# Attention and gated MLP on one core: bias rows mirrored in the matmul, splits and some relus given to POOL, and a new instruction order planned with a corrected count

## The chip, the cores and the metric

The kernel runs on one core of one Trainium2 chip. That core has five engines with their own instruction queues: TensorE (PE in the profile, its weight loads PEld), VectorE (DVE), ScalarE (ACT), GpSimd (POOL) and SyncE (SP, which issues DMA transfers here). They share the on-chip memory SBUF; matmul results land in PSUM. The metric is device time in microseconds of one execution, lower is better. Three timed runs of the kernel before gave 770.35, 771.11 and 771.43 us.

## What is computed

Eight batches, eight heads, 576 positions, head size 64. Attention with a position bias from a small two-layer network, then a gated MLP over the 512 joined channels. Cut to what matters:

```python
scores = scale * np.matmul(q, k.transpose(0, 1, 3, 2))
psi_rel = np.log1p(np.abs(rel)); psi_i = np.log1p(np.maximum(pos[:, None], 1.0))
h = np.maximum((psi_rel / psi_i)[..., None] @ w1 + b1, 0.0)      # 32 hidden
scores = scores + (h @ w2).transpose(2, 0, 1)[None]              # a bias per head
attn = softmax(scores);  x = attn @ v                            # heads joined to 512 channels
gate = sigmoid(causal 5-tap convolution of x, per channel)
out = (gate * (x @ w_val)) @ w_out
```

The bias of row i at column j depends on |i - j| and on i alone, so a row of it is a function of the distance, laid out forwards from the diagonal and backwards before it.

## The kernel before

**An order worked out on the host.** Nothing is scheduled by hand or by a compiler. While the kernel is built, every piece of work is entered as a task with `add`: the engines that may do it with a cost for each, a priority, the tasks it needs, and the buffers it takes and uses. `Plan.order` then plays the program through in a model of the five engines, and emits the tasks in the order that this gives, each on the engine that the model chose. What steers it are tables of numbers at the top of the file: `PAIR_AT` and `MLP_AT` (when a pair of heads, or an MLP, is due), `OFFS` (priority by kind of task), `LOOK` (how far a task may jump the queue for a buffer), `LOAD` (how an engine's time is weighed). `RUNS` sets in which order the 32 pairs (two heads of a batch) come. For TensorE the model also counts instructions: `INSTR` holds how many each kind of task issues, and each time the count passes `BLOCK` = 256 the model lets TensorE wait until a block of instructions has been fetched.

**Bias rows** (`bias_rows`, 36 calls, m = 0 to 35, 16 rows i each). Four `relu` tasks (ACT L348, DVE or POOL L350) make the hidden layer for the w distances that these rows need (288 to 576). `bias_mm` (L370) multiplies it in TensorE, four 32-row groups side by side, in one or two column pieces. `bias_fin` (ACT L390, DVE L392) takes each piece out of PSUM into `t_be` once forwards and once backwards (a reversed output pattern), two to four evictions for each m. `bias_store` sends `t_be` to DRAM, from where `bias_ld` (L442, L446) reads it skewed, so that the bias of a chunk of 128 rows is in place.

**Pairs** (`pair`, 32). For each of five chunks of rows: `qkm` or `qkr` (PE L843, L863) makes scores, `logits` (DVE L714) adds the bias and takes the minimum, `expo` (ACT L727), `eps`, `recip`, and `norm` (POOL L740). Then the weights are turned: for the first four pairs by TensorE (`tp`, `tpr`, `tpe`, evicted by ACT or DVE copies L260, L262), for the others by DVE (`turn_`, L887, L889). `av` (PE L944) multiplies with v in three tasks of 48 matmuls; a matmul of 32-bit operands is two matmuls and two weight loads in the trace, so such a task is 96 of each. `ev` (L268, L270) moves the result to `xp`.

**MLPs** (`mlp`, 8, one for each batch when its four pairs are done). `conv` and `sig` make the gate. In two parts of positions (256 and 320): `split_hi` (L260, L262, L264) and `split_lo` (L273) split x into two 16-bit numbers, `val` (PE L1082, three groups of four matmuls for each of four column blocks), `gf` (DVE L1092), `ghi` and `glo` (L260 to L264 and L273) split the gated product, `outp` (PE L1145), `ote`, and a store.

**Scales.** `wm_fin` takes the maxima of both weight matrices on DVE (`all_max`, once for each), and `vm_fin` those of v for each batch.

Of the kernel before, what the change touches and what calls it, by code (L numbers as in the profile page):

```python
# [50 lines left out]
INSTR = dict(qkm=16, qkr=32, av=192, bias_mm=16, val=8, outp=8, vm_sum=4, tp=16, tpr=4, tpe=10, avt=16)  # L51
# [167 lines left out]
def attention_gated_mlp(  # L219
# [105 lines left out]
    def bias_rows(m):  # L325
# [7 lines left out]
        cuts = (0, w) if w <= 512 else (0, w // 2, w)  # L333
# [31 lines left out]
        def bias_mm(e, j):  # L365
            if j == 0:
                new(pb, [P, 2, 512], F32)
            x, y = pieces[j]
            for g in range(4):
                T.matmul(  # L370
                    pb.t[32 * g : 32 * g + 32, j, 0 : y - x],
                    lhsT=w28,
                    rhs=rel[g].t[:, x:y],
                    start=True,
                    stop=True,
                    tile_position=(0, 32 * g),
                )

        def bias_fin(e, j, lo, hi, back):
            if j == 0 and not back:  # L380
                new(be, [P, S + 16], F32)
            x = pieces[j][0]
            i = pb.t[:, j, lo - x : hi - x]
# [1 line left out]
            if back:
                o = be.t[:, wb - hi : wb - lo][:, ::-1]
            else:
                o = be.t[:, wb - 1 + lo : wb - 1 + hi]
# [5 lines left out]
        fs, bs = [], []  # L394
        first = t = None
        for j, (x, y) in enumerate(pieces):
            t = add([("P", 0.1 + 0.5 * (y - x) / HS)], partial(bias_mm, j=j), rts + [t], pri + 0.3, [pb] if j == 0 else (), [rel[0]])
            for back, n, l in ((False, wf, fs), (True, wb, bs)):
                lo, hi = max(x, 1 if back else 0), min(y, n)
                if lo >= hi:  # L400
                    continue
# [855 lines left out]
```

## Time and profile before

| | |
|---|---|
| timed runs | 770.35, 771.11, 771.43 us; median 771.11 |
| the profiled execution | 773.37 us, of which the span from first to last instruction is 771.6 |
| busy in that span | PE 642.9, DVE 614.3, ACT 561.6, POOL 483.5 us |
| mean granted TensorE clock | 0.957 of full |
| DMA | 142 MB, 184 GB/s |

A busy time is the union of an engine's instructions. "Idle before, releaser" says how long the engine stood idle just before a group, and what ended it; "issue" as the releaser means that the profile shows nothing that the engine waited for. The program has three parts: some 70 us in which the bias rows are made, a stretch to about 280 us in which the weights are prepared and the first pairs run, and then the steady work, with the last pair's `av` ending at 729.4 us and the last MLP behind it.

### The profile page before, as it was taken

What the parts mean: (1) busy time and instruction counts of PE and PEld (TensorE: products, weight loads), DVE (VectorE), ACT (ScalarE), POOL (GpSimd) and SP (SyncE); (2) the same over time, 40 slices, a digit from 0 to 9 for tenths busy, and PEclk for the clock granted to TensorE, in tenths of its full rate; (3) what the DMA queues carried; (4) which work ended last, traced back from release to release, by engine and by line L of the source; (5) the groups of instructions that cost most, each with busy time, mean ns of one, the idle gap of its engine ahead of it and who ended that gap; (6) DMA issues with size and microseconds to landing.
All of it is one profiled execution on the core that took longest, in us unless ns stands there. A gap on an engine that the chain in (4) does not pass through costs nothing. (4 is left out here: it accounts for less than half of the span.)

```text
span 771.6 us, 27070 instructions
## 1 busy us (share of the span) xinstructions
PE 642.9 (83%) x11244; PEld 403.6 (52%) x11244; DVE 614.3 (80%) x1392; ACT 561.6 (73%) x1315; POOL 483.5 (63%) x567
## 2 busy tenths in 40 slices
PE   5667898878577899898988899899889999778976
PEld 1123555455364556565565475557546565555643
DVE  6998889898976779979886988879688896977420
ACT  6998787878755587879757876788488485677532
POOL 0200568786953795869867777768588377667541
PEclk9899999986888999999999999999999999899999
DMA  8999955694576455773768147654764456920011
GB/s 276 308 341 299 304 183 181 216 280 131 162 252 179 131 177 152 216 230 100 236 199 256 43 137 233 224 190 125 242 203 146 144 171 204 287 84 16 17 56 41
DMA packets 57642, 142.15 MB, mean 184 GB/s; under 512 B 6192, under 2 KB 6960, under 8 KB 57520
## 3 DMA queue, kind: packets, MB, share of 16 engines
q1 hardware_dynamic: 52272, 130.99, 54.1%
q10 hardware_dynamic: 5248, 9.44, 3.5%
q8 instruction: 88, 1.44, 0.8%
q14 instruction: 34, 0.28, 0.1%
HBM read 120.08 MB, written 20.33 MB: 182 GB/s over the span
## 5 line engine op out<-in xcount | busy, mean ns | idle before, releaser
L740 POOL TENSOR_SCALAR t_d<-t_d,rinv 128x576 f32<-128x576 f32 x256 | 201.3, 800 | 133.6 <-DVE rinv L736 129.6
L727 ACT ACTIVATE t_d<-t_d,nm 128x576 f32<-128x576 f32 x256 | 196.3, 767 | 54.6 <-DVE nm L714 41.5
L714 DVE CUSTOM_DVE_ANT_0 t_d<-t_sp,bias 128x576 f32<-128x576 f32 x256 | 186.3, 743 | 24.9 <-PE t_sp L843 21.2
L843 PE MATMUL t_sp<-t_qk 64*128 64x288 f32 x1024 | 169.4, 447 | 36.2 <-DVE nm L714 22.8
L944 PE MATMUL t_sp<-t_pt,t_vx 32*64 32x128 f32 (+1 forms) x8064 | 166.4, 301 | 27.5 <-issue 19.9
L944 PEld LDWEIGHTS t_sp<-t_pt,t_vx 32*64 32x64 f32 x8064 | 144.8, 135 | 54.9 <-issue 39.3
L887 DVE STREAM_TRANSPOSE t_pt<-t_d 128x1152 f32<-128x1152 f32 x112 | 152.0, 1365 | 12.8 <-POOL t_d L740 6.5
L1022 POOL TENSOR_TENSOR t_w<-t_w 128x576 f32<-128x576 f32 x96 | 136.8, 1429 | 14.1 <-ACT t_w L1017 7.9
L843 PEld LDWEIGHTS t_sp<-t_qk 64*128 64x128 f32 x1024 | 96.4, 195 | 90.4 <-DVE nm L714 33.8
L1082 PEld LDWEIGHTS <-wv 128*128 128x128 f16 x768 | 72.2, 99 | 48.4 <-issue 30.6
L1082 PE MATMUL t_sp<-xh,wv 128*128 128x320 f16 (+1 forms) x512 | 79.0, 291 | 7.9 <-DVE t_w L1092 4.9
L1145 PE MATMUL t_sp<-wo,gh 128*128 128x512 f16 x256 | 64.8, 385 | 12.8 <-ACT t_w L268 7.5
L268 ACT ACTIVATE xp<-t_sp,xsc 128x256 f32<-128x256 f32 (+1 forms) x108 | 38.6, 391 | 49.4 <-PE t_sp L944 45.5
L1092 DVE SCALAR_TENSOR_TENSOR t_w<-t_sp,wrel,t_w 128x256 f32<-128x256 f32 (+1 forms) x64 | 32.5, 510 | 41.4 <-PE t_sp L1082 36.0
L370 PE MATMUL t_sp<-rel,w 128*32 128x288 f32 (+17 forms) x352 | 44.0, 540 | 20.7 <-ACT t_be L390 11.0
L1017 ACT ACTIVATE t_w<-xp,convb 128x576 f32<-128x576 f32 x74 | 55.4, 767 | 5.3 <-DMA out<-t_w 2.5
L273 POOL TENSOR_TENSOR gl<-t_w,gh 128x256 f16<-128x256 f32 x48 | 33.0, 690 | 32.1 <-ACT gh L260 26.4
L1145 PEld LDWEIGHTS <-gh 128*128 128x128 f16 x256 | 23.5, 99 | 47.8 <-issue 18.8
L727 ACT ACTIVATION_READ_ACCUMULATOR t_d<-t_d,nm 128x1 f32 x256 | 47.9, 187 | 0.0
L348 ACT ACTIVATE rel<-gt,b1t,sct 128x432 f32<-128x432 f32 (+17 forms) x69 | 47.5, 763 | 0.0
L733 ACT ACTIVATE rinv<-sm,epst 128x2 f32<-128x2 f32 (+1 forms) x160 | 44.3, 287 | 1.8 <-ACT t_d L727 0.4
L1082 PE MATMUL t_sp<-xl,wv 128*128 128x256 f16 (+1 forms) x256 | 42.6, 289 | 2.6 <-DVE t_w L1092 1.9
(128 smaller groups left out, 833.4 us busy)
## 6 DMA issues: line engine op xcount, KB each, us to landing
bias<-bias_d SPq DMA_DIRECT2D x72, 576.0 KB, 5.5
t_vx<-vr SPq DMA_DIRECT2D x84, 384.0 KB, 3.7
t_qk<-qkd SPq DMA_DIRECT2D x32, 576.0 KB, 4.8
bias_d<-t_be SPq DMA_DIRECT2D x36, 295.5 KB, 4.8
t_vx<-vf SPq DMA_DIRECT2D x24, 384.0 KB, 3.6
out<-t_w ACTq DMA_DIRECT2D x32, 256.0 KB, 2.2
biasr<-bias_d SPq DMA_DIRECT2D x36, 144.0 KB, 6.7
t_d<-wvd SPq DMA_DIRECT2D x4, 512.0 KB, 6.7
```

Of the source, the lines that this page charges most:

```text
L348: A.activation(out=rel[g].t[:, 0:w], in_=src, func=AF.Relu, bias=b1t, scale=sct[:, mm : mm + 1])
L714: V.tensor_tensor_reduce(out=eb.t[:, a * S : (a + 1) * S].rearrange("p (j f) -> p j f", j=2), in0=sps[a].t[:, :, 0:HS], in1=bias.rearrange ...
L727: A.activation(out=x, in_=x, func=AF.Exp, bias=st["nm"][:, a : a + 1], scale=-1.0, accum_out=st["sm"][:, a : a + 1])
L733: A.activation(out=st["r"][:, 0:heads], in_=st["sm"][:, 0:heads], func=AF.Identity, bias=epst)
L740: (G if e == "G" else V).tensor_scalar(out=t, in0=t, scalar1=st["r"][:, a : a + 1], scalar2=1.0, op0=ALU.mult, op1=ALU.mult)
L843: T.matmul(ts[a][:, j, 0:HS], lhsT=qk.t[r, c * P : (c + 1) * P], rhs=qk.t[r, S + j * HS : S + (j + 1) * HS], start=True, stop=True,)
L887: V.transpose(out=x[:, c : 9 - c : 8 - 2 * c, :], in_=eb.t.rearrange("p (a f) -> p a f", a=2))
L944: T.matmul(avs[i // 2].t[o, i % 2, 0 : 32 * k], lhsT=vxs[j0 // 6].t[r, j - j0, o], rhs=pv[r, 0:k, j, :] if a == 0 else pv[r, 8 : 8 - k : - ...
L1017: A.activation(out=tmp.t, in_=x, func=AF.Copy, scale=cw)
L1022: (V if e == "V" else G).tensor_tensor(out=gates[k].t, in0=gates[k].t, in1=tmp.t, op=ALU.add)
L1082: T.matmul(pm.t[:, d % 2, 0:w], lhsT=pools["wv"][wi][:, k, d * P : (d + 1) * P], rhs=xb.t[xi][:, k, 0:w], start=(q == 0 and k == 0), stop= ...
L1145: T.matmul(pm.t[:, y, :], lhsT=gb.t[gi][:, k, o : o + P] if o < 256 else gx.t[gi][:, k, :], rhs=pools["wo"][wi][:, k, :], start=(q == 0 an ...
```

## The change

It has these parts.

1. `bias_mm` writes the whole row of 592 columns to PSUM, the backward half by reading `rel` with a reversed pattern (`[:, ::-1]`), in three or four pieces (`cuts`), and one `bias_fin` evicts it whole.
2. Every fourth m gives its fourth `relu` to POOL alone (`ON_G`), and POOL's modelled cost falls from 2.6 to 1.9 us for 576 columns.
3. `INSTR` of the tasks that turn weights on TensorE is raised by a fraction (`tp` 16 to 16.75, and so on): the model's count was short by what they issue besides matmuls and loads.
4. `all_max` takes both weight matrices at once; `vm_fin` makes two scale rows with one instruction (`xsc`, `osc`, `vmx` are laid out for it).
5. Modelled costs of `ev`, `norm`, `wm_fin`, `vm_fin` are altered, `av` and `ev` get a due time of their own (`PAIR_B`), so does the second part of an MLP (`MLP_B`), and all tables are set anew. With that the whole order is another.

```diff
-PAIR_AT = (12, -16, -1, -7.5, -6.5, -5.5, 7.5, -19.5, 9, -8, -4.5, 2.5, 3.5, 2, -3, -4.5, -4, 2.5, 2.5, -2.5, 3.5, -8.5, -5.5, -8.5, -3, -7, -2, -21.5, -19.5, -2.5, -2.5, 20)
+PAIR_AT = (15, -17.5, 2, -11.5, -6.5, -24, -8.5, -5, 10, -17, -4.5, -3.5, -8.5, 4, 8.5, 5.5, 0.5, -1.5, -4.5, -13.5, -13, -2.5, -2.5, -6, -4.5, -12, -10, -15.5, -4.5, 13, 29, 24.5)
...
-INSTR = dict(qkm=16, qkr=32, av=192, bias_mm=16, val=8, outp=8, vm_sum=4, tp=16, tpr=4, tpe=10, avt=16)
+INSTR = dict(qkm=16, qkr=32, av=192, bias_mm=16, val=8, outp=8, vm_sum=4, tp=16.75, tpr=4.75, tpe=10.75, avt=16.45)
...
-LOAD = dict(P=0.8, V=1.07, A=0.48, G=0.68, S=1.61)
+LOAD = dict(P=0.49, V=2, A=0.74, G=1.15, S=1.8)
...
+ON_G = tuple(range(0, 36, 4))
...
-        cuts = (0, w) if w <= 512 else (0, w // 2, w)
+        left = int(wf > wb)
+        mid = wb - 1 + left
+        cuts = sorted({0, mid, SPLIT, 2 * SPLIT})
...
-            eng = [("A", 0.22 + 0.54 * w / S), ("V", 0.1 + 0.4 * w / S), ("G", 0.15 + 2.6 * w / S)]
+            eng = [("A", 0.22 + 0.54 * w / S), ("V", 0.1 + 0.4 * w / S), ("G", 0.15 + 1.9 * w / S)]
+            if g == 3 and m in ON_G:
+                eng = eng[2:]
...
+        def bias_mm(e):
+            new(pb, [P, 2, 512], F32)
+            for x, y in pieces:
+                if y <= mid:
+                    lo, hi = mid - y + 1, mid - x + 1
+                else:
+                    lo, hi = x - mid, y - mid
+                for g in range(4):
+                    r = rel[g].t[:, lo:hi]
+                    T.matmul(
+                        pb.t[32 * g : 32 * g + 32, x // SPLIT, x % SPLIT : x % SPLIT + y - x],
+                        lhsT=w28,
+                        rhs=r[:, ::-1] if y <= mid else r,
...
+        t = add([("P", 0.1 + 0.04 * len(pieces) + 1.03)], bias_mm, rts, pri + 0.3, [pb], [rel[0]], times=len(pieces))
+        f = add([("A", 0.59), ("V", 0.72)], bias_fin, [t], pri + 0.5, [be], [pb])
...
-        for x in range(2):
-            V.tensor_reduce(out=wall[:, x : x + 1], in_=i[:, x], op=ALU.max, axis=AX.X)
-            all_max(wall[:, x : x + 1])
+        V.tensor_reduce(out=wall[:, 0:2], in_=i, op=ALU.max, axis=AX.X)
+        all_max(wall[:, 0:2])
...
-                ta = add([("P", 1.62)], partial(av, j0=j0), turned + [tvs[j0 // 6], ta], s0 + 13, () if ta else avs, u)
+                ta = add([("P", 1.62)], partial(av, j0=j0), turned + [tvs[j0 // 6], ta], s0 + 13 + PAIR_B[n], () if ta else avs, u)
...
-            base = st + (12 + 9 * pi) * per
+            base = st + (12 + 9 * pi) * per + pi * MLP_B[done]
```

What the order makes of it is shown at three places. Line numbers of the changed kernel are about ten lower than before: its L354 and L356 are `relu`, L396 and L398 `bias_fin`, L717 `expo`, L730 `norm`, L277 the splits, L833 `qkm`, L934 `av`, L1135 `outp`.

The first is ACT's queue where the bias rows end and the first softmax begins; `t_be` is a bias row on its way to DRAM, `t_d` a chunk of weights. Before:

```order
L348 ACTIVATE rel<-gt,b1t,sct 128x560
L348 ACTIVATE rel<-gt,b1t,sct 128x576
L390 ACTIVATE t_be<-t_sp,cadd 128x80
L348 ACTIVATE rel<-gt,b1t,sct 128x576
L390 ACTIVATE t_be<-t_sp,cadd 128x511
L390 ACTIVATE t_be<-t_sp,cadd 128x264
L390 ACTIVATE t_be<-t_sp,cadd 128x271
L390 ACTIVATE t_be<-t_sp,cadd 128x279
L390 ACTIVATE t_be<-t_sp,cadd 128x16
L390 ACTIVATE t_be<-t_sp,cadd 128x287
L727 ACTIVATE t_d,sm<-t_d,nm 128x576 x3
L733 ACTIVATE rinv<-sm,epst 128x2
```

Now:

```order
L396 ACTIVATE t_be<-t_sp,cadd 128x592
L354 ACTIVATE rel<-gt,b1t,sct 128x528 x2
L354 ACTIVATE rel<-gt,b1t,sct 128x544 x2
L717 ACTIVATE t_d,sm<-t_d,nm 128x576
L354 ACTIVATE rel<-gt,b1t,sct 128x560 x2
L354 ACTIVATE rel<-gt,b1t,sct 128x576
L717 ACTIVATE t_d,sm<-t_d,nm 128x576
L354 ACTIVATE rel<-gt,b1t,sct 128x576
L723 ACTIVATE rinv<-sm,epst 128x2
L717 ACTIVATE t_d,sm<-t_d,nm 128x576 x3
L723 ACTIVATE rinv<-sm,epst 128x2
L396 ACTIVATE t_be<-t_sp,cadd 128x592
```

The first five exponentials stand ahead of ACT's last bias eviction, among its last rectifications, where before all of the bias work came first.

The second is TensorE's queue late in the program, between the pairs that come 29th and 30th: `t_pt` are turned weights, `t_vx` is v, `gh` an MLP's gated product. An `av` run of two tasks is 73 rows that alternate between two widths, of which the last three or four are shown. Before:

```order
L944 MATMUL t_sp<-t_pt,t_vx 64x160 x2
L944 MATMUL t_sp<-t_pt,t_vx 64x128
L944 MATMUL t_sp<-t_pt,t_vx 64x160
L944 MATMUL t_sp<-t_pt,t_vx 64x128
L843 MATMUL t_sp<-t_qk 128x288 x12
L944 MATMUL t_sp<-t_pt,t_vx 64x160
L944 MATMUL t_sp<-t_pt,t_vx 64x128
```

Now, behind the run of two `av` tasks of the 30th pair:

```order
L934 MATMUL t_sp<-t_pt,t_vx 64x160
L934 MATMUL t_sp<-t_pt,t_vx 64x128
L934 MATMUL t_sp<-t_pt,t_vx 64x160
L833 MATMUL t_sp<-t_qk 128x288 x4
L1135 LDWEIGHTS gh
L1135 MATMUL t_sp<-wo_1271,gh 128x512
```

Before, another run of two `av` tasks followed behind three `qkm`; now one `qkm` and an MLP's output product stand behind the run.

The third is POOL's queue in the first MLP: `t_w` and `gh`, `gl` are the gated product and its two halves, `xh`, `xl` those of x. Before:

```order
L264 TENSOR_SCALAR gh<-t_w 128x256 x2
L273 TENSOR_TENSOR gl<-t_w,gh 128x256 x2
L740 TENSOR_SCALAR t_d<-t_d,rinv 128x576 x2
L273 TENSOR_TENSOR gl<-t_w,gh 128x256
L740 TENSOR_SCALAR t_d<-t_d,rinv 128x576
L273 TENSOR_TENSOR xl<-xp,xh 128x320 x2
L740 TENSOR_SCALAR t_d<-t_d,rinv 128x576 x2
L273 TENSOR_TENSOR xl<-xp,xh 128x320
```

Now:

```order
L277 TENSOR_TENSOR da<-da,wo_1271 128x512
L611 TENSOR_TENSOR wo_1272<-da,dm 128x512
L268 TENSOR_SCALAR xh<-xp 128x320
L277 TENSOR_TENSOR xl<-xp,xh 128x320 x4
L730 TENSOR_SCALAR t_d<-t_d,rinv 128x576 x2
L730 TENSOR_SCALAR t_w<-t_w,rinv 128x576
L730 TENSOR_SCALAR t_d<-t_d,rinv 128x576 x3
L277 TENSOR_TENSOR gl<-t_w,gh 128x256
L277 TENSOR_TENSOR gxl<-t_w,gxh 128x64
```

The part of 320 positions now comes first, and all four of its `xl` stand on POOL (three before, with one on DVE). Over the whole program no `xl`, `gl` or `gxl` is left on DVE, where 25, 16 and 8 were.

## Rows read from the trace of the kernel before

**Rows 1.** Part 1 of the page: engine, busy us, share, instructions.

```profile
PE 642.9 (83%) x11244; PEld 403.6 (52%) x11244; DVE 614.3 (80%) x1392; ACT 561.6 (73%) x1315; POOL 483.5 (63%) x567
```

**Rows 2.** Windows: stretch, length, busy of five engines, PE clock, DMA share, GB/s.

```profile
0.00:70.00 70.00, 44.73 (x364) 14.03 (x366) 59.88 (x166) 62.70 (x113) 5.44 (x8) 0.93 0.92 310
70.00:280.00 210.00, 167.33 (x2545) 110.60 (x2544) 178.50 (x414) 151.67 (x371) 142.16 (x158) 0.91 0.65 201
280.00:640.00 360.00, 325.35 (x6459) 211.24 (x6447) 302.95 (x662) 272.14 (x668) 262.87 (x320) 0.99 0.58 182
```

**Rows 3.** Part 4 of the page: the chain that ended last, by engine.

```profile
PE 28%; ACT 6%; DVE 5%; issue 3%; DMA 1%; POOL 0%; ACTq 0%; DVEq 0%
```

**Rows 4.** Timeline of PE: start, us, instruction, count, idle before and releaser.

```profile
683.69 1.88 PE L944 MATMUL t_sp<-t_pt,t_vx 32*64 32x160 f32 x92 [1.22 <-issue]
685.49 1.20 PE L863 MATMUL t_sp<-t_qk 64*64 64x288 f32 x16
686.62 0.75 PE L944 MATMUL t_sp<-t_pt,t_vx 32*64 32x160 f32 x20
688.12 1.60 PE L944 MATMUL t_sp<-t_pt,t_vx 32*64 32x160 f32 x76 [0.75 <-issue]
```

**Rows 5.** Part 3 of the page: queue, packets, MB, share of the DMA engines.

```profile
q8 instruction: 88, 1.44, 0.8%
```

**Rows 6.** Waits of PE: us in total, times, longest us.

```profile
PE t_sp L944 <- issue: 19.9, 15, 3.0
```

**Rows 7.** Groups by line, 0 to 72 us: busy, mean ns, idle before.

```profile
L348 ACT ACTIVATE rel<-gt,b1t,sct 128x432 f32<-128x432 f32 (+17 forms) x69 | 47.5, 763 | 0.0
...
L350 DVE TENSOR_SCALAR rel<-gt,sct,nb 128x560 f32<-128x560 f32 (+17 forms) x72 | 32.1, 505 | 0.9 <-PE t_sp L370 0.6 <-DMA gt<-grel 0.3
L390 ACT ACTIVATE t_be<-t_sp,cadd 128x264 f32<-128x264 f32 (+37 forms) x43 | 19.3, 493 | 1.6 <-DMA bias_d<-t_be 0.8 <-PE t_sp L370 0.8
L392 DVE TENSOR_SCALAR t_be<-t_sp,cadd 128x288 f32<-128x288 f32 (+32 forms) x37 | 16.7, 477 | 3.6 <-DMA bias_d<-t_be 2.0 <-ACT t_be L390 1.4
...
L350 POOL TENSOR_SCALAR rel<-gt,sct,nb 128x432 f32<-128x432 f32 (+2 forms) x3 | 5.1, 1684 | 26.2 <-PE t_sp L370 24.6 <-DMA bias_d<-t_be 1.5
```

**Rows 8.** Groups by form: bias evictions of four widths (271 is a backward one).

```profile
L390 ACT ACTIVATE t_be<-t_sp,cadd 128x272 f32<-128x272 f32 x2 | 1.0, 484 | 0.0
L390 ACT ACTIVATE t_be<-t_sp,cadd 128x271 f32<-128x271 f32 x2 | 1.0, 481 | 0.0
L392 DVE TENSOR_SCALAR t_be<-t_sp,cadd 128x495 f32<-128x495 f32 x1 | 0.7, 726 | 0.0
...
L390 ACT ACTIVATE t_be<-t_sp,cadd 128x512 f32<-128x512 f32 x1 | 0.7, 692 | 0.0
```

**Rows 9.** Timeline of DVE: start and end of one `all_max`.

```profile
23.26 0.18 DVE L514 COPY am<-wall 128x32 f32<-128x32 f32 x1
...
25.40 0.16 DVE L560 TENSOR_REDUCE wall<-wsc 128x1 f32<-128x4 f32 x1
```

**Rows 10.** Windows of line L273 alone (the splits): busy of DVE, of POOL.

```profile
0.00:280.00 280.00, 2.72 (x4) 17.09 (x22) 0.91 0.72 228
...
sum 772.00, DVE 29.57 POOL 76.87; mean DVE 9.86 POOL 25.62
```

**Rows 11.** Groups by form, whole program: a split on each engine, two DVE groups.

```profile
L262 DVE COPY t_pt<-t_sp 128x512 f32<-128x512 f32 x16 | 10.7, 684 | 2.9 <-ACT t_pt L260 2.8
L273 DVE TENSOR_TENSOR xl<-xp,xh 128x256 f16<-128x256 f32 x17 | 10.4, 621 | 0.0
...
L273 POOL TENSOR_TENSOR xl<-xp,xh 128x256 f16<-128x256 f32 x15 | 10.2, 693 | 1.2 <-ACT xh L260 1.2
...
L473 DVE TENSOR_SCALAR da<-dt 128x512 int32<-128x512 int32 x8 | 5.6, 705 | 0.0
```

**Rows 12.** Timeline of POOL and DVE from 172 us.

```profile
172.14 1.40 POOL L1022 TENSOR_TENSOR t_w<-t_w 128x576 f32<-128x576 f32 x1
...
172.50 1.32 DVE L473 TENSOR_SCALAR da<-dt 128x512 int32<-128x512 int32 x1
```

More of the change, by code (lines that the diff above doesn't have):

```diff
@@ L363, in bias_rows, with bias_fin @@
             )
[L365 to L383, printed above, removed]
+        def bias_mm(e):
[11 more added lines that the diff above has]
+                        rhs=r[:, ::-1] if y <= mid else r,
+                        start=True,
+                        stop=True,
+                        tile_position=(0, 32 * g),
+                    )
+        def bias_fin(e):
+            o = new(be, [P, 2 * SPLIT], F32).rearrange("p (j f) -> p j f", j=2)
+            i = pb.t[:, :, 0:SPLIT]
             cb = cadd[:, sum(full) : sum(full) + 1]
[L385 to L388, printed above, removed]
             if e == "A":
@@ L392, in bias_fin @@
                 V.tensor_scalar(out=o, in0=i, scalar1=cb, scalar2=None, op0=ALU.add)
[L394 to L401, printed above, removed]
-                f = add(
-                    [("A", 0.2 + 0.19 * (hi - lo) / 288), ("V", 0.1 + 0.31 * (hi - lo) / 288)],
-                    partial(bias_fin, j=j, lo=lo, hi=hi, back=back),
-                    [t, first],
-                    pri + 0.5,
-                    [be] if first is None else (),
-                    [pb],
-                )
-                first = first or f
-                l.append(f)
+        t = add([("P", 0.1 + 0.04 * len(pieces) + 1.03)], bias_mm, rts, pri + 0.3, [pb], [rel[0]], times=len(pieces))
+        f = add([("A", 0.59), ("V", 0.72)], bias_fin, [t], pri + 0.5, [be], [pb])
         def bias_store(e):
@@ L572, in wm_fin @@
         V.tensor_scalar(
[L573 removed]
+            out=wall[:, 3:], in0=wsc[:, 0, :, 1], scalar1=wall[:, 0:1], scalar2=2.0**-15, op0=ALU.mult, op1=ALU.mult
         )
         V.tensor_scalar(out=wsc[:, :, :, 1], in0=wsc[:, :, :, 1], scalar1=2.0**9, scalar2=None, op0=ALU.mult)
[L577 removed]
+    wfin = add([("V", 5.2)], wm_fin, wmax, -2)
     wfree = [closed]
@@ L633, in attention_gated_mlp @@
             wdone = weight(src.bitcast(I32)[k * P : (k + 1) * P, :], DM, hi_lo, k, wdone, 14 + 16 * i + 4 * k)
-    xsc = [cp.tile([P, 2, NK], F32, name=f"xsc_{b}") for b in range(B)]
-    osc = [cp.tile([P, 4], F32, name=f"osc_{b}") for b in range(B)]
+    xsc = [cp.tile([P, NK], F32, name=f"xsc_{b}") for b in range(B)]
+    osc = [cp.tile([P, 1 + NK], F32, name=f"osc_{b}") for b in range(B)]
+    vmx = [cp.tile([P, 4], F32, name=f"vmx_{i}") for i in range(2)]
     convb = [cp.tile([P, NK, TAPS], F32, name=f"convb_{i}") for i in range(2)]
@@ L753, in soft @@
         t = add([("V", 0.08)], recip, [t], h + heads + 0.5)
-        nr = [add([("G", 0.75)], partial(norm, a=a), [t], h + heads + 0.6 + a / 2) for a in range(heads)]
+        nr = [add([("G", 0.79)], partial(norm, a=a), [t], h + heads + 0.6 + a / 2) for a in range(heads)]
         return eb, nr
@@ L929, in pair @@
                 d = turned + tvs + [ta]
-                ta = add([("P", 0.96 * kn)], partial(avt, k0=k0, kn=kn), d, s0 + 13, () if ta else avs, u, times=kn)
+                ta = add([("P", 0.96 * kn)], partial(avt, k0=k0, kn=kn), d, s0 + 13 + PAIR_B[n], () if ta else avs, u, times=kn)
         else:
```

55 lines of the change are left out of this document (28 added, 27 removed).

## The prediction

> **What bounds the kernel now.** Read the busy times first: TensorE works 643 us of 772, VectorE 614, ScalarE 562, POOL 484 [rows 1]. No engine is full, so ask where each is. The windows by stage answer it [rows 2]. Up to 70 us ScalarE (62.7 of 70) and VectorE (59.9) carry the bias rows, while the DMA engines are 92% busy at 310 GB/s and TensorE has 25 us to spare. From 70 to 280 us VectorE is the fullest, 178.5 of 210 (85%), TensorE 167 (80%). From 280 to 640 us TensorE has 325 of 360 (90%) and VectorE 84%. [...]
>
> The chain of waits says the same of the later part [rows 3]: its shares add to 43% of the span, so it reaches back some 330 us from the end, and 28 of the 43 are TensorE, 6 ScalarE, 5 VectorE, POOL nothing. In it stands an odd item, "issue" with 3%: TensorE waits for nothing that the profile can name. The timeline shows it inside runs of `av` [rows 4]: idle 1.22 us, then 92 + 16 + 20 = 128 matmuls, then idle 0.75. With a weight load each that is 256 instructions from stall to stall. The instruction queue moved 88 packets of 1.44 MB together, 16.4 KB each [rows 5], which is 256 instructions of 64 bytes, and 88 × 256 is about the 22,488 matmuls and loads that TensorE has [rows 1]. So TensorE waits for its next block of code where it runs through one faster than the next arrives. The waits of `av` for "issue" are 15, 19.9 us together, the longest 3.0 [rows 6]: 1.3 us each.
>
> [...]
>
> **Part by part.** All sums are made against the profiled execution, 773.37 us, which is 2.26 above the median 771.11.
>
> *Bias rows.* VectorE had 72 `relu` for 32.1 us and 37 evictions for 16.7 [rows 7]. Now it has 56 (505 ns wide, but the wide ones stay, so 24.9 by their widths) and 15 whole rows. One of 495 took 726 ns [rows 8]; 592 should take about 0.83, so 12.4 us. With the maxima that is 7.2 + 4.3 + 2.1 = 13.6 us less; the 2.1 is one `all_max`, 23.26 to 25.40 [rows 9], of which one falls away. ScalarE had 69 `relu` (47.5) and 43 evictions (19.3) [rows 7]; now 75 and 21. An eviction of 512 took 692 ns [rows 8], so 592 some 0.78, 16.4 us together, and the added relus eat the gain: about 67 us before and after. ScalarE was at 62.7 of 70 and remains what the stage waits for; besides, the DMA engines are at 0.92 [rows 2]. POOL takes 13 relus for 3, at 1.7 us for 432 columns [rows 7], up to 2.2 for 576: 17 to 22 us more, on an engine with 5.4 busy of 70 [rows 2]. TensorE writes 36 × 592 = 21,312 columns where it wrote 15,840, so its 44 us become at most 59 of the 70. Whether a reversed operand costs TensorE more no row shows. The nearest is a reversed output on ScalarE, 481 ns for 271 columns beside 484 for 272 forwards [rows 8], so nothing; if it doubled, half of those columns (the backward ones) would add some 20 us to 59, and TensorE would set this stage, about 9 us longer. I take nothing, by the near row, and keep the 9 for the range. Fewer pieces also mean fewer hand-overs, and the first exponentials come before the last relus. **Bias stage: −3, between −7 and +9.** The lower end is half of VectorE's 13.6: the other half is spare time already.
>
> *70 to 280 us.* Two things leave VectorE here: the four splits (2.7 us [rows 10]) and 7 copies of turned weights (684 ns [rows 11], 4.8 us, to ScalarE with 152 of 210). That is 7.5 us of its 178.5, and it also comes out of the bias stage up to 10 us ahead. If VectorE alone sets the pace, 17.5 us are gained; if TensorE's 167 and the transfers of weights (DMA 0.65) do, none. TensorE is only five points behind, so most of it is lost on it. **−6, between −17 and 0.**
>
> *Code blocks.* I took a block boundary that the trace shows as a stall and counted on by 256 in both orders. A block stalls when nearly all of it is `av`, the quickest instructions. Before, 12 blocks have at most eight others in the part where TensorE sets the pace; now five, two of them of `av` alone. Four more lie between 80 and 180 us, where VectorE is late anyway and they cost little. The mechanism is the order's second place: the run of `av` is followed by other work where the boundary falls. Seven fewer × 1.3 us [rows 6] = 9; those with eight others still wait a little, so I take **−8, between −13** (ten fewer) **and −2** (the count is wrong by a few and the stalls only wander). What follows such a stall is the end of `av`, and `ev`, `conv`, then `val` of the MLP; near the end that is the chain, so it is worth its full length there.
>
> *Splits on POOL.* Over the whole run VectorE gives up its 29.6 us of L273 [rows 10], and a few casts come back. POOL takes 49 splits at 0.69 at most (the small `gxl` less) [rows 11], up to 34 us. With the relus, and what it hands over in products and casts, its 484 become about 527; from 280 to 640 us its 263 [rows 2] become some 285 of 360, 79%. VectorE at 84% was not the bound there, so its relief counts for little. But POOL takes its tasks in turn, and `norm` releases the turning of weights, and that `av`. Two prices: a norm that stands behind a split waits 0.69 us for it, and the two engines get in each other's way: beside POOL's 1.40 us product a VectorE instruction of 705 ns [rows 11] took 1.32 [rows 12], 0.6 more. Fewer two-engine splits could also help, but I see no row for it. Weighed by slack (POOL still has a fifth), **+3, between 0 and +8.**
>
> *Nothing:* the tail. The last pair's `av` and the last MLP's products stand in the same order in both, and the new scale rows (one instruction for two) are far under 1 us a batch.
>
> Sum: −3 − 6 − 8 + 3 = −14, so 773.4 − 14 = 759.4 in a profiled execution, and 2.3 less, **757 us**, in the median.
>
> **Rivals.**
> *The stalls stay.* Part 3 doesn't do what it says: the model's count is still off, or the stall goes with what runs in the next block and not with this one. For: it needs a count right to a few in 23,600. Against: the positions in the trace all agree modulo 256. Then −14 + 8 = −6, and another 2 if four new ones bite: 764 to 769.5, say 766. [...]
>
> *VectorE was the bound early.* All 17 us show, and the rest as above: −3 − 17 − 8 + 3 = −25, 746, between 740 and 750. For: 85% [rows 2], and scores wait for `logits`. Against: TensorE 80% there.
>
> *Nothing moves.* Each relief meets the engine next to it; 769.6 to 772.7.
>
> *Slower: POOL becomes the bound.* Place: the steady pairs, where 28 of 32 turn their weights on VectorE and need the norms first. Price: one split of 0.69 us in front of the norms of each pair [rows 11], 28 × 0.69 = 19 us, with another 5 from blocked VectorE instructions (8 × 0.6). Against gains of 17 it decides from 17 / 28 = 0.6 us a pair. For: it is in turn, and three products of 1.4 us an MLP column stand there too. Against: POOL doesn't appear in the chain [rows 3] and keeps 75 us free of 360. 773.4 + 24 − 17 − 2.3 = 778; 772.7 to 785.
>
> **How the numbers follow.** Forecast (750 to 764): 45%. Stalls stay: 20%. VectorE early: 15%. Nothing: 5%. Slower: 15%. 0.2%, 1.5 us, is about what a measurement of this kernel can tell from no change; so faster 80%, same 5%, slower 15%. The range leaves out the fast half of the third case and most of the last: 745 to 773. The reversed operand at +9 gives 769 and lies in it.
>
> **What would show it.** Right, step by step: bias evictions of 592 columns, at about 0.8 us, and the first `logits` some 3 us earlier than before; L934 waiting for "issue" under 12 us in total (19.9 before); VectorE under 84% from 70 to 280; no split on VectorE; POOL near 527 us busy and still absent from the chain. Wrong: matmuls of the mirrored half longer per column than the forward half; as many "issue" stalls as before, elsewhere; long waits of VectorE's turns for `norm`; or TensorE idle in the steady part by as much as the stalls lost, for VectorE's or ScalarE's sake.

## The result: 744 us, 13 below the forecast and just below its range

The changed kernel took 743.85 us (median of four runs) against 771.0 beside it; the ratio is 0.9618, interval 0.9544 to 0.9693, so 29 us less, between 24 and 35. Forecast were 757, range 745 to 773. The sign was right, the size about half. Its profiled execution took 746.14 us (span 744.3), 27 less than that of before. One of the four runs was disturbed (835 us) and is left out of the ratio; the three others lie between 736.9 and 746.14.

The page after, parts 1, 3 (the instruction queue) and 4 (the chain):

```profile
PE 643.4 (86%) x11756; PEld 417.3 (56%) x11756; DVE 573.9 (77%) x1275; ACT 570.5 (77%) x1321; POOL 523.7 (70%) x611
...
q8 instruction: 92, 1.51, 0.8%
...
PE 42%; DVE 20%; ACT 18%; DMA 9%; issue 8%; POOL 1%; SPq 1%; ACTq 0%; DVEq 0%; POOLq 0%
```

TensorE is busy as long as before (642.9, [rows 1]), so the 27 us are all idle time of TensorE: 128.7 us before (771.6 − 642.9), 100.9 now. VectorE has 40 us less, POOL 40 more. The chain now reaches back over the whole span, and POOL has 1% of it. The windows say where the idle time went. First the last stretch of the kernel before (131.6 us of it lie in the span), then the changed kernel in the stretches of [rows 2] and in the last one (104.3 us):

```profile
640.00:810.00 170.00, 105.47 (x1897) 67.77 (x1895) 72.93 (x153) 75.10 (x167) 73.00 (x83) 0.96 0.24 75
```

```profile
0.00:70.00 70.00, 51.11 (x862) 30.49 (x864) 52.61 (x128) 63.14 (x98) 26.34 (x18) 0.98 0.93 315
70.00:280.00 210.00, 168.60 (x2450) 110.61 (x2445) 172.65 (x392) 156.17 (x385) 144.18 (x164) 0.89 0.62 198
280.00:640.00 360.00, 334.46 (x6883) 219.04 (x6881) 295.95 (x643) 289.55 (x695) 283.24 (x342) 0.99 0.62 192
640.00:810.00 170.00, 89.21 (x1570) 57.13 (x1568) 52.68 (x116) 61.66 (x144) 69.96 (x88) 0.99 0.17 55
```

TensorE's idle time fell by 6.4 us in the first 70 us, where it also has more to do, by 1.3 in the next 210, by 9.1 between 280 and 640, and by 11.0 behind that. So three quarters of the gain came after 280 us.

What TensorE waited for between 280 and 640 us, before (us in total, times, longest):

```profile
PE t_sp L843 <- DVE nm L714: 6.5, 8, 1.4
PE t_sp L944 <- issue: 5.5, 6, 2.2
PE t_sp L944 <- DVE nm L714: 3.0, 3, 1.4
PE t_sp L1082 <- issue: 2.8, 2, 2.0
```

and after:

```profile
PE t_sp L1072 <- DVE t_w L1082: 4.0, 6, 0.8
PE t_sp L1135 <- ACT t_w L272: 3.9, 7, 2.0
PE t_sp L934 <- issue: 2.4, 2, 1.6
...
PE t_sp L833 <- issue: 0.7, 1, 0.7
...
PE t_sp L833 <- DVE nm L704: 0.4, 2, 0.2
...
PE t_sp L934 <- DVE nm L704: 0.2, 1, 0.2
```

Two things went: the waits for code, 8.3 to 3.1 in these rows, and the waits of scores and `av` for `logits` on VectorE, 9.5 to 0.6. Other waits grew, so that the idle time fell by 9.1 in all. The forecast had the first; for the second it had nothing in this stretch.

The bias stage after, by line up to 72 us (answers to [rows 7] and [rows 8]):

```profile
L354 ACT ACTIVATE rel<-gt,b1t,sct 128x576 f32<-128x576 f32 (+17 forms) x75 | 50.9, 750 | 0.8 <-PE t_sp L382 0.8
...
L356 DVE TENSOR_SCALAR rel<-gt,sct,nb 128x544 f32<-128x544 f32 (+17 forms) x56 | 26.5, 523 | 6.3 <-PE t_sp L382 5.3 <-ACT rel L354 0.5 <-DMA gt<-grel 0.4
L356 POOL TENSOR_SCALAR rel<-gt,sct,nb 128x320 f32<-128x320 f32 (+11 forms) x13 | 25.9, 1997 | 39.3 <-PE t_sp L382 26.2 <-ACT rel L354 5.8 <-DMA gt<-grel 4.9
L396 ACT ACTIVATE t_be<-t_sp,cadd 128x592 f32<-128x592 f32 x20 | 14.7, 741 | 0.3 <-PE t_sp L382 0.3
L398 DVE TENSOR_SCALAR t_be<-t_sp,cadd 128x592 f32<-128x592 f32 x15 | 12.1, 827 | 0.3 <-DMA bias_d<-t_be 0.2
```

An eviction of 592 columns takes 741 ns on ScalarE and 827 on VectorE, where 0.78 and 0.83 were reckoned. A reversed operand costs TensorE nothing here. The width 199 occurs only mirrored and 200 only forwards, and one matmul takes 332 and 339 ns (the number before it is the time in which any of the eight ran):

```profile
L382 PE MATMUL t_sp<-rel,w 128*32 128x199 f32 x8 | 1.0, 332 | 0.0
...
L382 PE MATMUL t_sp<-rel,w 128*32 128x200 f32 x8 | 0.7, 339 | 0.0
```

All splits of x and of the gated product are now on POOL (answers to [rows 11]):

```profile
L277 POOL TENSOR_TENSOR gl<-t_w,gh 128x256 f16<-128x256 f32 x64 | 44.5, 698 | 24.4 <-ACT gh L264 23.7 <-DVE gh L266 0.5
L277 POOL TENSOR_TENSOR xl<-xp,xh 128x320 f16<-128x320 f32 x32 | 24.7, 795 | 1.1 <-ACT xh L264 1.1
L277 POOL TENSOR_TENSOR xl<-xp,xh 128x256 f16<-128x256 f32 x32 | 23.1, 736 | 0.7 <-PE t_sp L1072 0.7
```

### The profile page after: what moved, and what is told of

Same layout as the page of the kernel before. It is cut to its first block, busy times and chain, and to the rows that moved or that the text cites. A ratio compares the mean times of both kernels' runs of the same rounds, so it can differ in the third digit from the quotient of the medians.

```text
span 744.3 us, 28072 instructions
## 1 busy us (share of the span) xinstructions
PE 643.4 (86%) x11756; PEld 417.3 (56%) x11756; DVE 573.9 (77%) x1275; ACT 570.5 (77%) x1321; POOL 523.7 (70%) x611
## 4 chain that ended last, share of the span: by engine, by line
PE 42%; DVE 20%; ACT 18%; DMA 9%; issue 8%; POOL 1%; SPq 1%; ACTq 0%; DVEq 0%; POOLq 0%
PE t_sp L934 12%; PE t_sp L833 10%; PE t_sp L1072 8%; PE t_sp L1135 6%; DVE t_d L704 6%; ACT t_d L717 5%; DVE t_pt L877 5%; DMA t_vx<-vf 4%; ACT rel L354 3%; DMA t_qk<-qkd 2%; ACT t_w L1027 2%; DVE t_w L1082 2%; PE t_sp L899 1%; DVE vmx L642 1%; ACT t_w L272 1%
## 5 line engine op out<-in xcount | busy, mean ns | idle before, releaser
L730 POOL TENSOR_SCALAR t_d<-t_d,rinv 128x576 f32<-128x576 f32 x256 | 198.9, 789 | 99.8 <-DVE rinv L726 93.5
L717 ACT ACTIVATE t_d<-t_d,nm 128x576 f32<-128x576 f32 x256 | 196.5, 768 | 59.2 <-DVE nm L704 50.2
L833 PE MATMUL t_sp<-t_qk 64*128 64x288 f32 x1024 | 170.3, 454 | 25.9 <-DVE nm L704 7.8
L934 PE MATMUL t_sp<-t_pt,t_vx 32*64 32x128 f32 (+1 forms) x8064 | 163.2, 300 | 19.5 <-issue 14.7
L934 PEld LDWEIGHTS t_sp<-t_pt,t_vx 32*64 32x64 f32 x8064 | 142.7, 134 | 42.7 <-issue 30.4
L833 PEld LDWEIGHTS t_sp<-t_qk 64*128 64x128 f32 x1024 | 96.5, 198 | 79.3 <-DVE nm L704 16.9
L1072 PE MATMUL t_sp<-xh,wv 128*128 128x256 f16 (+1 forms) x512 | 76.2, 289 | 8.0 <-DVE t_w L1082 5.8
L1135 PE MATMUL t_sp<-wo,gh 128*128 128x512 f16 x256 | 63.8, 380 | 8.6 <-ACT t_w L272 6.9
L1007 ACT ACTIVATE t_w<-xp,convb 128x576 f32<-128x576 f32 x79 | 59.3, 765 | 4.5 <-DMA out<-t_w 1.5
L382 PE MATMUL t_sp<-rel,w 128*32 128x296 f32 (+37 forms) x864 | 50.0, 354 | 14.5 <-ACT rel L354 8.8
L1082 DVE SCALAR_TENSOR_TENSOR t_w<-t_sp,wrel,t_w 128x320 f32<-128x320 f32 (+1 forms) x64 | 31.8, 506 | 38.8 <-PE t_sp L1072 36.3
L277 POOL TENSOR_TENSOR gl<-t_w,gh 128x256 f16<-128x256 f32 x64 | 44.5, 698 | 24.4 <-ACT gh L264 23.7
L356 POOL TENSOR_SCALAR rel<-gt,sct,nb 128x320 f32<-128x320 f32 (+11 forms) x13 | 25.9, 1997 | 39.3 <-PE t_sp L382 26.2
L354 ACT ACTIVATE rel<-gt,b1t,sct 128x576 f32<-128x576 f32 (+17 forms) x75 | 50.9, 750 | 0.8 <-PE t_sp L382 0.8
L277 POOL TENSOR_TENSOR xl<-xp,xh 128x320 f16<-128x320 f32 (+1 forms) x64 | 47.8, 765 | 1.8 <-ACT xh L264 1.1
L382 PEld LDWEIGHTS t_sp<-rel,w 128*32 128x32 f32 x864 | 29.3, 115 | 35.1 <-ACT rel L354 16.2
L717 ACT ACTIVATION_READ_ACCUMULATOR t_d<-t_d,nm 128x1 f32 x256 | 48.1, 188 | 0.0
```

Source lines behind the costliest of these rows:

```text
L277: (V if e == "V" else G).tensor_tensor(out=out, in0=in0, in1=in1, op=ALU.subtract)
L354: A.activation(out=rel[g].t[:, 0:w], in_=src, func=AF.Relu, bias=b1t, scale=sct[:, mm : mm + 1])
L382: T.matmul(pb.t[32 * g : 32 * g + 32, x // SPLIT, x % SPLIT : x % SPLIT + y - x], lhsT=w28, rhs=r[:, ::-1] if y <= mid else r, start=True, ...
L717: A.activation(out=x, in_=x, func=AF.Exp, bias=st["nm"][:, a : a + 1], scale=-1.0, accum_out=st["sm"][:, a : a + 1])
L730: (G if e == "G" else V).tensor_scalar(out=t, in0=t, scalar1=st["r"][:, a : a + 1], scalar2=1.0, op0=ALU.mult, op1=ALU.mult)
L833: T.matmul(ts[a][:, j, 0:HS], lhsT=qk.t[r, c * P : (c + 1) * P], rhs=qk.t[r, S + j * HS : S + (j + 1) * HS], start=True, stop=True,)
```

## Experiments

Times are compared by their ratio to the kernel before, run beside each; 0.01 is 7.7 us. The changed kernel itself and two variants of it that do as well (`after_256`, `after_relu_back`) have 0.9618, 0.9627 and 0.9624, so 0.962 is the mark. Of eighteen kernels ten keep an order and change one thing in it, one of them three; eight are planned anew.

### The blocks of code, with the order kept

One-column matmuls in the bias stage move all later block boundaries; nothing else in the order changes. Two of them go in front of each m's own, for so many m that there are 64, 28 or 8 (56 for the kernel before); one is four instructions.

```diff
         def bias_mm(e):
             new(pb, [P, 2, 512], F32)
+            for _ in range(2 if 2 <= m < 34 else 0):
+                T.matmul(pb.t[0:32, 0, 0:1], lhsT=w28, rhs=rel[0].t[:, 0:1], start=True, stop=True, tile_position=(0, 0))
             for x, y in pieces:
```

> The changed kernel with 64 one-column matmuls added in its bias stage, two for each of 32 rows m, which are 256 instructions of TensorE more; the order of all else stays. A whole block of code is added, so every later block boundary falls where it fell. This is the control of the next run. Both theories: as the changed kernel (744 us, ratio 0.962 to before) or up to 3 us later, since TensorE has 19 us to spare in that stage; stalls of av for issue as before it, 15 us.

> The same with 28 such matmuls, 112 instructions: every later boundary falls 112 instructions earlier in the order than in the changed kernel, while nothing else moves. By a count along the order 14 more blocks then hold nearly nothing but av. Theory (stalls belong to blocks, and the corrected count laid the order on them): 14 more stalls of about 1.2 us, 13 to 20 us slower than the run with 256, waits of av for issue above 28 us. Rival (a stall goes with the work around it, or the gain came from elsewhere): within 3 us of the run with 256.

> The changed kernel with eight one-column matmuls in its bias stage, 32 instructions, and nothing else: every later block boundary falls 32 instructions earlier in the order, which by a count along it gives as many stalls as before had. Theory (stalls of code are the largest of the three terms put back): 11 to 17 us slower than the changed kernel, 754 to 761. Rival (the three together cost more than each, stalls alone little): under 8 us, 743 to 751.

Measured: 742.37 us (0.9627, 0.9533 to 0.9721); 774.42 (1.0058, 1.0018 to 1.0099); 751.21 (0.9756, 0.9714 to 0.9798). With the blocks in the wrong place, the changed kernel is slower than the one before: 112 instructions cost 33 us. 32 of them cost 10 (between 6 and 15), a little less than the 11 to 17 expected. The waits of `av` for "issue", in the run with 256 and then in the one with 112 (in each row the longest is not a wait for code, as the last section shows):

```profile
PE t_sp L936 <- issue: 16.5, 10, 7.3
```

```profile
PE t_sp L936 <- issue: 38.8, 24, 6.2
```

There are 14 more, as the count along the order said, and 22 us more. The time rose by 33, above the 13 to 20 expected. Of the 32.6 us between the two traces 17.8 are idle time of TensorE; the other 14.8 are busy time, 656.0 us for 641.2, for nearly the same work at a lower granted clock (0.954 for 0.969 in the mean). The timeline of TensorE in the run with 112 (start, us, instruction, count, idle before and releaser):

```profile
577.35 2.46 PE L936 MATMUL t_sp<-t_pt,t_vx 32*64 32x128 f32 x128 [0.19 <-issue]
584.39 1.37 PE L936 MATMUL t_sp<-t_pt,t_vx 32*64 32x128 f32 x29 [4.57 <-issue]
585.68 2.29 PE L835 MATMUL t_sp<-t_qk 64*128 64x288 f32 x8
587.91 3.20 PE L1137 MATMUL t_sp<-wo,gh 128*128 128x512 f16 x8
591.04 1.24 PE L835 MATMUL t_sp<-t_qk 64*128 64x288 f32 x8
```

and windows there (length, busy of five engines, clock, DMA share, GB/s):

```profile
582.00:586.00 4.00, 1.61 (x31) 1.18 (x33) 0.17 (x1) 0.16 (x1) 2.15 (x3) 0.72 0.51 190
586.00:590.00 4.00, 4.00 (x13) 1.61 (x12) 3.19 (x4) 3.24 (x8) 0.00 (x0) 0.50 0.35 102
```

A block of 128 matmuls runs in 2.46 us, then TensorE stands for 4.57. Behind that the granted clock is 0.50, where it was 1.00 from 574 to 582 us. Eight matmuls of a score task take 2.29 us there and 1.24 a little later.

> The kernel before with 64 one-column matmuls in its bias stage, 256 instructions, boundaries unmoved: the control of the next run. Both theories: 771 to 774 us, waits of av for issue about 20 us.

> The kernel before with 56 of them, 224 instructions, so that every later boundary falls 32 instructions later than before. That is by how much the count of its planner was off, so its order now lies on the blocks as its planner meant it. By a count along the order 8 of its 12 stalling blocks get other work in. Theory: 7 to 11 us faster than the run with 256 (762 to 766), waits of av for issue 8 to 11 us. Rival (the stalls only wander, or what follows takes the time): within 2 us of it.

Measured: 773.4 us (1.0048, 1.0010 to 1.0085) and 764.77 (0.9931, 0.9891 to 0.9972), 0.0117 or 9 us apart, as expected. So the order of before had been laid for blocks that lay 30 instructions elsewhere, and put on them it gains 9 us without any other change. The "issue" row of `av` falls less than I expected, from 21.5 to 17.4. But 6.2 us of such waits on other lines are gone too, and the rows hold waits for VectorE (last section): those for code alone, on all lines, fall from 20.6 to 12.3 us.

### The splits, with the order kept

Just before the tasks are emitted, the engine of the splits is overwritten: in the kernel before all of them go to POOL; in the changed kernel the 41 tasks that VectorE did in the kernel before go back to it.

```diff
     for t in todo:
+        if getattr(t.fn, "func", t.fn).__name__ in ("split_lo", "glo"):
+            t.on = "G"
         t.fn(t.on)
```

> The kernel before, order and all else as it was, but the 41 tasks of splits (25 xl, 16 gl with 8 gxl) that VectorE did are done by POOL at the same place of the order. Theory (VectorE's relief pays in the steady part, which the prediction left out): waits of scores for logits fall from 23 to about 12 us, 5 to 9 us faster. Rival (POOL becomes the bound, norms queue behind splits): 3 to 10 us slower, turns of VectorE wait longer for norm. Third (both or neither): within 2 us.

> The changed kernel, order as it is, but the same 41 tasks go back to VectorE at the same place of the order. Theory: the waits of scores for logits rise from 8 to about 18 us, 5 to 10 us slower than the changed kernel (749 to 754). Rival (POOL is the dearer place, or VectorE has room): 0 to 5 us faster.

Measured: 768.06 us (0.9967, 0.9931 to 1.0004) and 747.53 (0.9724, 0.9640 to 0.9809). By the middle values POOL is the better place both ways: 2.5 us gained in the old order (not clear of zero), some 8 lost in the new one (its interval allows 1 to 15 against the mark; against the three runs of the changed kernel alone it holds zero). The first fell short of the 5 to 9 us expected. The scores' waits for `logits` over the whole program, first in the kernel before with its splits on POOL (22.8 without), then in the changed kernel with them on VectorE (7.8 without), moved less than the 12 and 18 that I expected:

```profile
PE t_sp L843 <- DVE nm L714: 19.4, 26, 2.1
```

```profile
PE t_sp L833 <- DVE nm L704: 13.1, 15, 2.0
```

The scores' wait for `logits` between 280 and 640 us rises from 0.4 to 2.6 in the changed kernel with the splits on VectorE:

```profile
PE t_sp L833 <- DVE nm L704: 2.6, 6, 0.7
```

So the rival that POOL becomes the bound falls. The splits are a third of the fall from 6.5 to 0.4 (2.2 of 6.1), and of that over the program (5.3 of 15.0). The rest came with the order; no run takes it apart.

### The bias stage

> The changed kernel, order as it is, with nine rectifications of ScalarE in the bias stage done twice, some 6.5 us more work on the engine that this stage waits for: first logits at 72 us, where before had them. Theory (the stage's earlier end reaches the end of the program): 4 to 7 us slower than the changed kernel, 748 to 751. Rival (the stretch to 280 us has slack that takes it up): within 2 us, 742 to 745.

> The changed kernel, order as it is, with the 13 rectifications that POOL does in the bias stage given back to VectorE and ScalarE in turn. Theory (VectorE and ScalarE are loaded in this stage, but its end doesn't reach the end of the program): first logits 3 to 6 us later, total 0 to 3 us slower. Rival (POOL's relief matters): 4 us slower or more.

In the first, the first rectification of ScalarE is issued twice for every fourth m; in the second, POOL's 13 go to VectorE and ScalarE in turn; the order is kept.

```diff
                 full.append(1 << g)
+                if len(full) == 1 and m % 4 == 2:
+                    A.activation(out=rel[g].t[:, 0:w], in_=src, func=AF.Relu, bias=b1t, scale=sct[:, mm : mm + 1])
```

Measured: 742.49 us (0.9660, 0.9565 to 0.9756) and 741.36 (0.9624, 0.9585 to 0.9663). The first `logits` in the kernel before, the changed one and the delayed one:

```profile
70.82 0.76 DVE L714 CUSTOM_DVE_ANT_0 t_d<-t_sp,bias 128x576 f32<-128x576 f32 x1
```

```profile
65.25 0.76 DVE L704 CUSTOM_DVE_ANT_0 t_d<-t_sp,bias 128x576 f32<-128x576 f32 x1 [0.54 <-PE t_sp L833]
```

```profile
70.95 0.76 DVE L706 CUSTOM_DVE_ANT_0 t_d<-t_sp,bias 128x576 f32<-128x576 f32 x1 [0.54 <-PE t_sp L835]
```

The stage ends 5.6 us earlier than before. Given back (5.7 later), half of it shows at the end, 0.0037 or 3 us, but the interval, −5 to 11, allows all or nothing. The traces speak for nothing: the 101st of the 288 `logits` starts at 265.5 us in the delayed run, at 268.4 in the changed kernel and at 264.7 in the run with 256, so the stretch to 280 us had taken the delay up. With POOL's rectifications given back the first `logits` come 2.7 us later (67.9), and nothing that can be measured is left at the end.

### All three put back, with the new order kept

> The changed kernel's order with three things put back: the 41 tasks of splits on VectorE, ScalarE's 6.5 us more in the bias stage, and 32 instructions of TensorE more there, so that by a count along the order its stalls of code are those of before. Theory (these three are all of the gain): 766 to 774 us. Rival (the order itself holds 8 us or more): 752 to 763.

It joins the splits on VectorE, the doubled rectifications and 32 instructions. Measured: 763.56 us (0.9956, 0.9913 to 0.9998). Of the 0.038 that the change gained, 0.033 are gone (26 us), and 0.0044 (3 us) remains against before, less than the rival wanted. Alone the three cost 0.0133, 0.0101 and 0.0037, together 0.027; jointly they cost a little more, within the uncertainty, which is 0.006 to 0.010 for each single difference. On top of the 32 instructions alone (0.9756) the splits and the later bias stage cost 0.0200, 15 us, between 11 and 20.

So in the new order these three cost nearly as much as the change gained. They do not bring the waits of before back, though. The waits for code do return, 19.0 us (18.9 before, 8.5 in the changed kernel, by the last section's reading). TensorE's waits for `logits`, all its lines, stay at 16.9 us, where before had 33.9 and the changed kernel has 16.6; the rest of the time lies in TensorE's busy time (6.1 us more than in the changed kernel) and in the bias stage. So the times agree better than the waits do.

### Parts planned anew

> The kernel before with the new bias rows alone (mirrored matmuls, whole evictions, every fourth m with a relu on POOL), its order planned by the old tables, which moves the later work a little too; by a count along the order its stalls of code are some 3 us more. Theory (the bias stage gives what the changed kernel shows in it): the first logits at 66 to 67 us instead of 71.6, and of that 2 to 5 us are left at the end. Rival (the stage ends no earlier, ScalarE holds it): first logits at 71 us or later, total within 2 us or slower.

> The changed kernel with its new code, costs and count, but planned by the tables of before: PAIR_AT, MLP_AT, OFFS, LOAD as they were, the due times for the later parts of pairs and MLPs at zero. By a count along the order its stalls are some 3 us more than in the changed kernel. Theory (most of the gain beyond the stalls comes from where the tables put the work, VectorE's splits with it): 756 to 768 us. Rival (the new code brings the gain and the tables only a little): 744 to 752 us.

> The changed kernel with one part undone: INSTR of the tasks that turn weights is as it was, so the planner counts some 30 instructions too few again; the tables are the new ones and the order is planned anew. By a count along the order the stalls of code are 2.3 times those of the changed kernel (10 blocks more with little but av). Theory (the count is worth what the shifted runs showed, about 2 us for each such block): 760 to 768 us, waits of av for issue above 25 us. Rival (the order is what counts, and it changes anyway): outside that range on either side, the issue waits not to blame.

> The kernel before with one part alone: the new INSTR, all tables and code as before, the order planned anew. By a count along the order its stalls are two thirds of those of before. Theory of the count: 3 to 8 us faster than before. Rival (tables that were fitted to one count don't fit another order): no faster than before, or slower by up to 20 us, with longer waits for logits or for other engines.

> The changed kernel with the separate due times for av, ev and the second part of an MLP taken away (PAIR_B and MLP_B zero), all else new; planned anew. By a count along the order its stalls are as many as in the run shifted by 112. If stalls are all that differ: 770 to 778 us. Theory of the fitted order: 780 us or more, the rest above that in other waits.

> The changed kernel with one due time moved: the eleventh entry of PAIR_AT from -4.5 to -2.5. The order is planned anew and differs in places; by a count along it the stalls of code are those of the changed kernel. Theory (the order as a whole is fitted, and any other order gives some of it away): 748 to 765 us. Rival (the order is sturdy; what counts is the count and the cheaper work): 741 to 747 us.

> The changed kernel with another due time moved, the 25th entry of PAIR_AT from -4.5 to -3.5, planned anew; stalls by count as in the changed kernel. Theory (fitted to the point, any move costs): 760 us or more. Rival (the first nudge happened on a bad order): 741 to 750.

> The kernel before with the eleventh entry of PAIR_AT moved by 2 as in the first nudge (-4.5 to -2.5), planned anew; stalls by count 1.7 us more than before. Theory (the old order is fitted no less): 790 us or more. Rival (the old order was less fitted, so its tables bear a change): 766 to 780.

The edits are as told in these lines; that of the first nudge stands for them:

```diff
-PAIR_AT = (15, -17.5, 2, -11.5, -6.5, -24, -8.5, -5, 10, -17, -4.5, ...
+PAIR_AT = (15, -17.5, 2, -11.5, -6.5, -24, -8.5, -5, 10, -17, -2.5, ...
```

| planned anew | us | ratio, interval |
|---|---|---|
| before_new_bias | 787.9 | 1.0258, 1.0186 to 1.0330 |
| after_old_tables | 803.34 | 1.0442, 1.0381 to 1.0502 |
| after_old_count | 795.03 | 1.0358, 1.0282 to 1.0434 |
| before_new_count | 768.28 | 0.9980, 0.9940 to 1.0020 |
| after_no_due_b | 852.5 | 1.1076, 1.0994 to 1.1158 |
| after_nudge | 787.78 | 1.0254, 1.0197 to 1.0310 |
| after_nudge_2 | 749.92 | 0.9792, 0.9712 to 0.9871 |
| before_nudge | 766.45 | 0.9994, 0.9961 to 1.0028 |

Four came out slower than expected (`before_new_bias`, `after_old_tables`, `after_old_count`, `after_nudge`), and mostly not for the stalls of code: TensorE's waits for `logits` over the program are 36.9 to 52.8 us in them, for 16.6 in the changed kernel and 33.9 before. `after_old_count` has 16 us more of waits for code besides. In `before_new_bias` the first `logits` come at 41.5 us, because its order puts them ahead of the end of the bias rows, so they don't tell when that stage ended. In `before_new_count` the waits for code fell from 18.9 us to 13.3, as the count wanted, but those for `logits` and for `xp` on ScalarE grew by 13 together. `after_no_due_b` fell out as the theory of the fitted order wanted; `after_nudge_2` and `before_nudge` went to their rivals. The first nudge has as many stalling blocks by count as the changed kernel and takes 49 us more by its ratio; the second takes 13 more, while the old order bears such a nudge for nothing. The windows from 500 to 640 us, first the changed kernel, then the nudged one:

```profile
500.00:640.00 140.00, 133.73 (x2907) 88.51 (x2906) 118.92 (x262) 116.64 (x281) 111.66 (x138) 1.00 0.64 198
```

```profile
500.00:640.00 140.00, 121.11 (x2557) 81.31 (x2542) 102.56 (x220) 98.14 (x237) 104.06 (x132) 0.96 0.49 156
```

Up to 500 us both had done nearly the same work (TensorE 420 and 417 us busy). From there every engine is less busy in the nudged kernel, and TensorE waits again for `logits`; its timeline:

```profile
514.18 1.24 PE L833 MATMUL t_sp<-t_qk 64*128 64x288 f32 x8 [0.47 <-DVE nm L704]
517.52 2.29 PE L833 MATMUL t_sp<-t_qk 64*128 64x288 f32 x8 [2.09 <-DVE nm L704]
```

No engine is full there, so I read it as a ring in which each waits for another; no run tests that. Behind a wait of 2.09 us the next score task takes 2.29 us for 1.24, as behind a stall of code. The parts of the change with the old tables are slower than before: tables and code are fitted to each other, and the parts can't be priced by planning anew. What in an order makes the ring tighten from one due time on was not settled.

## Why the prediction was half of it

*What bounds the kernel* held in the main: the stalls are blocks of 256 instructions (92 packets for 23,512 matmuls and loads after, 255.6 to a packet, as by [rows 5] and [rows 1] before; the 64 bytes that I named are 16.4 KB divided by 256, and no run shows them otherwise), and TensorE with its waits is the bound after 280 us. But three of the 15 waits in [rows 6], 6.1 of the 19.9 us and the longest among them, are not for code (last section), and those positions do not agree modulo 256. The other twelve are 13.8 us, 1.15 each. What such boundaries cost in this kernel depends on where they fall: moving them changed the time by 9, 10 and 33 us in the shifted runs.

*Bias stage, −3:* right in its mechanism, ScalarE's 67 us (50.9 + 14.7 = 65.6 after) with the operand read backwards for nothing (332 ns for 199 columns mirrored, 339 for 200 forwards). Its end came 5.6 us earlier; what of that is left at the end is not clear of zero.

*70 to 280 us, −6:* wrong. VectorE's busy time fell by 5.9 us there and TensorE's idle time by 1.3, near the end of the range that I gave as 0. Counted with the waits that the last section gives to VectorE, TensorE waited for its `logits` there for 21.5 us before and 22.1 after. The granted clock there fell, too, from 0.91 to 0.89.

*Code blocks, −8:* right in cause and size, 10 us in the new order (undone, 6 to 15) and 9 in the old (done alone, 5 to 13); TensorE's waits for code fell from 18.9 to 8.5 us. The forecast has no term for the clock: in the run with 112 TensorE was busy 14.8 us longer than in the one with 256, at a granted clock of 0.954 for 0.969, but in the run with 32, at 0.969, its busy time did not rise (641.5 us).

*Splits on POOL, +3:* this is the step that failed, with its sentence "VectorE at 84% was not the bound there, so its relief counts for little". The waits of scores for `logits` stood in the trace of before, 6.5 us of them between 280 and 640 us (shown above), and over the whole program the largest of all of TensorE's waits:

```profile
PE t_sp L843 <- DVE nm L714: 22.8, 26, 2.2
```

I took a busy share of 84% for slack, and gave the steady part no term for TensorE's waits for VectorE. Behind 280 us these waits, all lines, came to 18.5 us before and to 2.6 after: 16 us less where I forecast 3 more, 19 off. The stretch to 280 us (5 less gained than forecast) and TensorE's other waits behind it (6 us longer) took some of that back; with the bias stage and the code blocks, 2 to 3 us each above the forecast in the trace, the miss is 13. VectorE, in turn with TensorE, delayed it at 84%, long before it was full. How much of this the splits did is less sure. Moved alone they are worth some 8 us in the new order (1 to 15) and 2.5 in the old one, where I forecast 3 lost; in the trace they bring 3 of the 16 us of waits back. The rest came with the new order, for which I had no term beyond the code blocks, and its cause stays open. The price that I set on POOL did not show: it took 33.1 us more on the splits' line (110.0 for 76.9, [rows 10]) and 523.7 us in all, as reckoned (527), and has 1% of the chain.

*The tail, 0:* right; from the last `av` to the end of the span 42 us in both.

Of the signs that I named, the waits of L934 for "issue" came out at 14.7 us and not under 12. One of 6.9 us stands at 168 us and is not for code (last section); without it they are 7.8. And the 0.2% that I took a measurement to tell was too small: the changed kernel's runs lie over 1% apart.

*Rivals:* that the stalls stay and that POOL becomes the bound are both refuted by runs with the order kept. That VectorE was the bound gave 746, near the result, but for another stretch: it put the 17 us before 280 us, and they came behind it.

## What to carry to other kernels

Read an engine's worth from the waits that end on it, not from its busy share: VectorE, 84% busy between 280 and 640 us, held up the scores eight times there and `av` three times. Where an order is planned, first ask whether its count of instructions per block matches the trace, and test it by shifting the blocks with a few idle instructions, which leaves the order alone. A wait that stays with the same work under every shift, as the one of 6.2 to 7.3 us did here, is not one for code. And price the parts of such a change with the order kept; a plan made anew for each part measures the plan (a due time moved by 2 cost 49 us).

## What was not expected of the hardware

A block of code that came late cost more than its wait: behind 4.57 us of standing still the granted clock was 0.50, and the next score task took 2.29 us for 1.24. In the run with 112 instructions TensorE was busy 14.8 us longer than in the one with 256, besides 22 us more of these waits.

The longest wait that the profile calls "issue" in the changed kernel, 6.89 us, is not one for code. TensorE's row of it, and VectorE's last row ahead of it, in the changed kernel:

```profile
174.97 4.10 PE L934 MATMUL t_sp<-t_pt,t_vx 32*64 32x128 f32 x138 [6.89 <-issue]
174.79 0.08 DVE L704 DVE_READ_ACCUMULATOR2_ANT nm<- 128x1 f32 x1
```

in the run with 112 instructions:

```profile
175.25 8.80 PE L936 MATMUL t_sp<-t_pt,t_vx 32*64 32x128 f32 x337 [6.21 <-issue]
175.07 0.08 DVE L706 DVE_READ_ACCUMULATOR2_ANT nm<- 128x1 f32 x1
```

and a wait of the kernel before, the longest in [rows 6]:

```profile
212.19 6.77 PE L944 MATMUL t_sp<-t_pt,t_vx 32*64 32x128 f32 x234 [2.98 <-issue]
212.01 0.08 DVE L714 DVE_READ_ACCUMULATOR2_ANT nm<- 128x1 f32 x1
```

Each ends 0.10 us after VectorE's first `logits` behind its turning of weights. In all eight traces that keep the changed kernel's order it stands ahead of the same `av`, 6.2 to 7.3 us long, whether the block boundaries fall 0, 32 or 112 instructions earlier. And no code came: in the changed kernel the instruction queue moved no packet between 149.80 and 177.36 us. The other waits for "issue" of over 0.45 us, in the traces of before, after and the run with 112, end 1.2 to 1.6 us after a packet of that queue has landed, but for five more that again end 0.10 us after VectorE's `logits` (two of before, 1.72 and 1.38 us; one of after, 1.23; two of the run with 112, 1.42 and 0.64). So "issue" is the profile's word for what it can't name, and the landing of a packet tells which of these waits were for code. The sums of waits for code in this document follow this reading.
